# Attention in native float32 on row and column parts of the TensorE array, written as one piece a pair in program order

## The chip, the cores and the metric

The kernel runs on one core of one Trainium2 chip. The metric is the device time of one execution in microseconds (us). The engines that matter are TensorE (PE, with its weight loads shown apart as PEld), VectorE (DVE), ScalarE (ACT), GpSimd (POOL) and SyncE (SP, which only issues DMAs here). Each engine runs its own list of instructions in order and waits on semaphores of the others.

## What is computed

Three blocks follow each other: a linear attention with random features, a gated MLP with a shift in time ("moe"), and a second MLP with a convolution ("moe2"). The change is in the first:

```python
def _attn_ref(q, k, v, w_phi) -> np.ndarray:

    def phi(x):
        proj = np.einsum('bhsd,df->bhsf', x, w_phi)
        proj = proj - np.max(np.abs(proj), axis=-1, keepdims=True)
        return np.concatenate([np.exp(proj), np.exp(-proj)], axis=-1)
    q_p, k_p = (phi(q), phi(k))
    kv = np.einsum('bhsf,bhsd->bhfd', k_p, v)
    z = np.sum(k_p, axis=2)
    num = np.einsum('bhsf,bhfd->bhsd', q_p, kv)
    den = np.einsum('bhsf,bhf->bhs', q_p, z)[..., None] + 1e-06
    return (num / den).astype(np.float32)
```

There are 8 batches, 8 heads, 576 positions, 64 channels a head and 128 features, so 256 with both signs. The moe has 512 channels and 1024 hidden ones: `k = relu(xk @ w_k)`, `v = k*k @ w_v`, `r = sigmoid(xr @ w_r)`, output `r * v`. All is float32.

## The kernel before

Attention works on pairs of heads, `Pi` = 0 to 31, four pairs a batch. For a pair it does these steps on TensorE:

- **Projections** (`project`, lines 242 to 261; `front_k`, `front_q`): q and k of both heads lie transposed in one tile of 128 rows (64 channels a head) and 1152 columns. Nine blocks of 128 columns are multiplied with a block-diagonal weight, 256 output columns for both heads. `BANKS` names the blocks: 5 to 8 are k, 0 to 3 are q, 4 is half q and half k. VectorE takes the maximum of the absolute values (L260) and subtracts it (L265), ScalarE makes exp and exp of the negative (L274, L275, L283, L284).
- **Sums** (`sums`, line 304): `pkv` += k features (128 positions x 128 features as weights) times v with a column of ones (65 columns): 16 products, and 2 of 130 columns for the half block `kr`.
- **Transposes** (`queries`, line 326): the centred q projections are transposed into `pt`, and ScalarE makes the exponentials from there (L345, L346).
- **Numerators** (`numerators`, line 357): 65 weight columns (64 channels and the denominator) times 288 query columns, into `pn`; ScalarE copies them out.
- **`finish`** (line 396) makes reciprocals of the denominators, and `last` (line 410) broadcasts them with a matmul `pr` (L418) and multiplies into `xT`, which the moe reads.

A float32 matmul on this array comes as two records in the trace (two halves of the weights). From pair `NAT` = 6 on the projections, and from pair `NATN` = 8 on the numerators, are not done in float32: operands are split into a rounded part and a rest in the faster `float32r` format (`split`, lines 226 to 240: L235, L236; `queries`: L349, L351, L352; `sums`: L320, L321), and three `float32r` products take the place of one (L256 to L258, and three in L377). The sums stay float32.

The moe (`moe`, line 513 on) is cut into pieces of 12 matmuls of 288 columns by `yield`; each matmul product is also three `float32r` ones (`mm3`, L147 to L149, into `psk`, `psr`, `psv`). The main loop (line 578) steps the attention of a pair and hands out moe pieces by a credit, ten a pair from pair 9 on. The order on each engine is not the order of the code: the framework's scheduler interleaves all instructions, with priority for attention. `order` (line 298) ties only sums and numerators into a chain. After attention the rest of the moe runs, and then moe2 (`psh`, `pso`).

PSUM has eight banks of 2 KB a partition: three in pool `psm` (tag "mm", the moe's and early projections) and five in `psa` (tag "at", attention's).

Of the kernel before, what the change touches and what calls it, by code (L numbers as in the profile page):

```python
# [15 lines left out]
P = 128  # L16
# [6 lines left out]
XT = 6  # L23
# [3 lines left out]
NAT, NATN, PP = 6, 8, 5  # L27
# [17 lines left out]
def fused_kernel(ctx: ExitStack, tc: tile.TileContext, qk, va, wphi, ones2, mu, wk, wv, wr, win, wout, cw, out):  # L45
# [9 lines left out]
    def f(x):  # L55
        return x.bitcast(F32)
# [40 lines left out]
    wph = const.tile([P, 2 * FT], F32R, name="wph")  # L97
    wpl = const.tile([P, 2 * FT], F32R, name="wpl")
    V.tensor_copy(wph, wp0)
    V.tensor_tensor(wpl, wp0, f(wph), ALU.subtract)  # L100

# [52 lines left out]
    with ExitStack() as p1:  # L154
# [45 lines left out]
        loaded, xk, xq, vts = {}, {}, {}, {}  # L200
        KC0 = 512

        def load(Pi):
# [8 lines left out]
            xk[Pi] = (raw,)  # L212
# [5 lines left out]

        def load_half(Pi, k):
            b, p = divmod(Pi, NP)  # L220
            c = slice(KC0, W) if k else slice(0, KC0)
            raw = pool.tile([P, W - KC0], F32, tag="rqk", bufs=1, name="rqk")[:, :c.stop - c.start]
            G.dma_start(raw, qk[b, p, :, c])
            loaded[Pi, k] = raw

        def split(Pi, k):

            raw = loaded.pop((Pi, k))
            if k:
                xh = pool.tile([P, W], F32R, tag="xh", bufs=1, name="xh")  # L230
                xl = pool.tile([P, W], F32R, tag="xl", bufs=1, name="xl")
                xk[Pi] = (xh, xl)
            xh, xl = xk[Pi]
            c = slice(KC0, W) if k else slice(0, KC0)
            A.copy(xh[:, c], raw)  # L235
            V.tensor_tensor(xl[:, c], raw, f(xh[:, c]), ALU.subtract)  # L236
            if k:
                load_half(Pi, False)
            elif Pi + 1 < B * NP:
                load_half(Pi + 1, True)  # L240

        def project(Pi, js):
# [25 lines left out]
        def front_k(Pi):  # L268
            kp = []
            for js in BANKS[:2]:  # L270
                ps, mx = project(Pi, js)
                k_ = pool.tile([P, 2, 2, 2, FT], F32, tag="kp", bufs=2, name="kp")
                t = centred(ps, mx, 2, "tk", 1)
# [30 lines left out]
        def sums(Pi):  # L304
# [8 lines left out]
            if Pi < NATN:  # L313
                kvf = pool.tile([P, 2, 2, V1], F32, tag="kvh", bufs=2, name="kvf")
                A.copy(kvf, pkv)
                kvs[Pi] = (kvf,)
            else:
                kvh = pool.tile([P, 2, 2, V1], F32R, tag="kvh", bufs=2, name="kvh")
                kvl = pool.tile([P, 2, 2, V1], F32R, tag="kvl", bufs=2, name="kvl")
                A.copy(kvh, pkv)  # L320
                V.tensor_tensor(kvl, pkv, f(kvh), ALU.subtract)  # L321
                kvs[Pi] = (kvh, kvl)
# [3 lines left out]
        def queries(Pi, h):  # L326

            t = ts[Pi]
            if Pi < NATN:
                qf = pool.tile([P, 2, S], F32, tag=("qh", "ql")[h], bufs=1, name="qf")  # L330
                q_ = (qf,)
            else:
                qh = pool.tile([P, 2, S], F32R, tag="qh", bufs=1, name="qh")
                ql = pool.tile([P, 2, S], F32R, tag="ql", bufs=1, name="ql")
                q_ = (qh, ql)
            qs[h] = q_
            for o, w, tl in ((0, 384, ((1, 0), (1, 1), (2, 0))), (384, 192, ((2, 1), (0, 0)))):
# [3 lines left out]
                if Pi < NATN:  # L341
                    e = qf[:, :, o:o + w]
                else:
                    e = pool.tile([P, 2, 384], F32, tag="e", bufs=2, name="e")[:, :, :w]
# [392 lines left out]
```

## Time and profile before

| | |
|---|---|
| time, median of 3 runs | 1309.07 us (1306.95 to 1310.03) |
| span of the profiled execution, first to last instruction | 1306.5 us |
| granted TensorE clock | 1.00 of full speed throughout |
| busy PE, DVE, ACT, POOL | 1289.4, 877.0, 797.6, 161.3 us |

The page gives no time of its own for the profiled execution beside its span; the median of the runs is 2.6 us above that span. A busy time sums the records of an engine without counting overlap twice. TensorE's matmuls are pipelined: a record's duration is longer than the time until the next one starts, so the cost of a matmul in a run is read from one start to the next.

### The profile page before, as it was taken

How to read it: one execution, taken by the hardware profiler on the slowest of the kernel's cores; microseconds unless marked ns; L12 is line 12 of the kernel's file. 1: busy time of each engine (PE TensorE's matmuls, PEld its weight loads, DVE VectorE, ACT ScalarE, POOL GpSimd, SP SyncE). 2: the span in 40 equal slices, each digit the busy share in tenths (PEclk: the TensorE clock that was granted, in tenths of full speed). 3: DMA queues.
4: the chain of work that ended last, by engine and by line, in shares of the span. 5: the costliest groups of instructions: out<-in, count | busy, mean ns of one | idle time of the engine just before them, and what ended most of it. 6: DMA issues, size and time to landing. Idle time of an engine off the chain costs nothing.

```text
span 1306.5 us, 25891 instructions
## 1 busy us (share of the span) xinstructions
PE 1289.4 (99%) x9962; PEld 1269.2 (97%) x9962; DVE 877.0 (67%) x1629; ACT 797.6 (61%) x1832; POOL 161.3 (12%) x256
## 2 busy tenths in 40 slices
PE   8899999999999999999999999999999999999998
PEld 7679999999999999999999999999999999999998
DVE  7968887878788778778876844433663553644743
ACT  6877775757667666666775654424564564554653
POOL 6716500111111111011100000000000000000000
PEclk9999999999999999999999999999999999999999
DMA  7313312223332223223221004013102102102100
GB/s 252 116 50 111 106 49 66 73 81 87 100 93 67 86 79 107 74 78 96 79 68 48 21 20 147 19 63 140 64 11 73 41 33 73 37 37 73 37 38 37
DMA packets 74217, 95.76 MB, mean 73 GB/s; under 512 B 26988, under 2 KB 51696, under 8 KB 74096
## 3 DMA queue, kind: packets, MB, share of 16 engines
q1 hardware_dynamic: 60304, 66.26, 16.2%
q0 software_dynamic: 4944, 18.29, 4.7%
q10 hardware_dynamic: 8848, 9.57, 2.6%
q8 instruction: 79, 1.29, 0.4%
q14 instruction: 42, 0.34, 0.1%
HBM read 66.39 MB, written 27.26 MB: 72 GB/s over the span
## 4 chain that ended last, share of the span: by engine, by line
PE 91%; DVE 4%; DMA 2%; ACT 2%; issue 1%; POOL 1%; SPq 0%; DVEq 0%; ACTq 0%; POOLq 0%
PE pn L377 7%; PE pkv L311 6%; PE psh L147 5%; PE psh L148 5%; PE pso L148 5%; PE pso L149 5%; PE psh L149 5%; PE psk L147 5%; PE pso L147 5%; PE psk L149 5%; PE psk L148 5%; PE psv L148 5%; PE psv L149 5%; PE psv L147 5%; PE psr L147 2%; PE psr L149 2%
## 5 line engine op out<-in xcount | busy, mean ns | idle before, releaser
L311 PEld LDWEIGHTS pkv<-va,kp 128*128 128x128 f32 x1024 | 153.9, 191 | 7.5
L148 PE MATMUL psk<-ml,wkh 128*128 128x288 f32 x512 | 152.3, 298 | 0.6 <-DVE ml L492 0.6
L147 PE MATMUL psk<-mh,wkl 128*128 128x288 f32 x512 | 152.7, 299 | 0.0
L311 PE MATMUL pkv<-va,kp 128*128 128x65 f32 x1024 | 152.2, 251 | 0.0
L149 PE MATMUL psv<-kh,wvh 128*128 128x288 f32 x512 | 152.0, 297 | 0.0
L149 PE MATMUL psk<-mh,wkh 128*128 128x288 f32 x512 | 151.6, 296 | 0.0
L148 PE MATMUL psv<-kl,wvh 128*128 128x288 f32 x512 | 151.3, 296 | 0.0
L148 PE MATMUL psh<-xl,wih 128*128 128x288 f32 x512 | 151.1, 296 | 0.0
L147 PE MATMUL psv<-kh,wvl 128*128 128x288 f32 x512 | 150.7, 295 | 0.0
L147 PE MATMUL psh<-xh,wil 128*128 128x288 f32 x512 | 150.6, 296 | 0.0
L149 PE MATMUL psh<-xh,wih 128*128 128x288 f32 x512 | 150.1, 294 | 0.0
L148 PE MATMUL pso<-gl,woh 128*128 128x288 f32 x512 | 148.8, 295 | 0.0
L149 PE MATMUL pso<-gh,woh 128*128 128x288 f32 x512 | 148.7, 295 | 0.0
L147 PE MATMUL pso<-gh,wol 128*128 128x288 f32 x512 | 144.1, 293 | 0.0
L641 DVE SCALAR_TENSOR_TENSOR ct<-h,cw,ct 128x576 f32<-128x576 f32 x64 | 52.4, 819 | 98.0 <-ACT ct L640 97.7
L260 DVE TENSOR_REDUCE mx<-ps 128x4 f32<-128x512 f32 (+1 forms) x160 | 100.0, 628 | 21.5 <-PE ps L258 12.4
L265 DVE TENSOR_TENSOR t<-ps,mx 128x512 f32<-128x512 f32 (+1 forms) x160 | 99.7, 626 | 2.7 <-PE pt L340 2.2
L148 PEld LDWEIGHTS psk<-ml,wkh 128*128 128x128 f32 x512 | 96.2, 188 | 0.8 <-DVE ml L492 0.8
L147 PEld LDWEIGHTS psk<-mh,wkl 128*128 128x128 f32 x512 | 96.1, 188 | 0.4 <-POOL wvl L176 0.3
L149 PEld LDWEIGHTS psv<-kh,wvh 128*128 128x128 f32 x512 | 96.4, 188 | 0.0
L149 PEld LDWEIGHTS psk<-mh,wkh 128*128 128x128 f32 x512 | 96.3, 188 | 0.0
L149 PEld LDWEIGHTS psh<-xh,wih 128*128 128x128 f32 x512 | 96.2, 188 | 0.0
(123 smaller groups left out, 3668.4 us busy)
## 6 DMA issues: line engine op xcount, KB each, us to landing
va<-va SPq DMA_DIRECT2D x32, 325.0 KB, 3.7
x2s<-x SPq DMA_DIRECT2D x32, 288.0 KB, 2.3
x2r<-x2s ACTq DMA_DIRECT2D x32, 288.0 KB, 3.3
out<-ot SPq DMA_DIRECT2D x32, 288.0 KB, 2.1
rqk<-qk POOLq DMA_DIRECT2D x26, 320.0 KB, 3.7
rqk<-qk POOLq DMA_DIRECT2D x26, 256.0 KB, 3.0
raw<-wk SPq DMA_DIRECT2D x8, 512.0 KB, 5.5
raw<-wv SPq DMA_DIRECT2D x16, 256.0 KB, 3.0
```

The source lines that it names most:

```text
L147: T.matmul(ps, wl, xh, start=first, stop=False)
L148: T.matmul(ps, wh, xl, start=False, stop=False)
L149: T.matmul(ps, wh, xh, start=False, stop=last)
L260: V.tensor_reduce(mx, ps, axis=AX.X, op=ALU.max, apply_absolute_value=True)
L265: V.tensor_tensor(t, ps, mx.unsqueeze(3).to_broadcast([P, n, 2, FT]), ALU.subtract)
L311: order(T.matmul(o, k_, v_, start=(i == 0), stop=(i == len(prods) - 1)))
L377: order(T.matmul(pn, kv[a][:, c, h], q_[i][:, c, w], start=(n == 0), stop=(n == len(prods) - 1)))
L641: V.scalar_tensor_tensor(t, h[:, 1:S + 1], cw0[:, fc, 1:2], t, ALU.mult, ALU.add)
```

## The change

From pair `SW` = 6 on attention is done by new functions. All splitting is gone, and every product is float32 with tiles that cover a part of the array:

- `rows`: a projection of one head uses the 64 rows of its channels and 128 weight columns; the two heads lie in the two row halves and write different banks.
- `sums4`: each product is cut into four of 32 weight columns, which write 32 partitions each.
- `numerators4`: the 64 channels of the two heads are four strips of 32 columns; the denominators are products of their own (`pd`), with the last 32 of the 65 columns as weights.
- `block(Pi)` writes a pair's whole TensorE work as one piece: the broadcast of the pair before, the transposes of `Pi`, projections of k for `Pi + 2` and q for `Pi + 1`, sums of `Pi + 1`, numerators of `Pi`. The main loop hands out ten moe pieces behind it, and TensorE runs all of this in program order (`manual_schedule`); the other engines are still scheduled. `finish` comes at step `FS` = 4 of 15.
- Pairs up to 5 stay as they are, and pair 6's projections are made by the old code over full rows, in float32.

```diff
-NAT, NATN, PP = 6, 8, 5
+SW, PP = 6, 5
+NS, FS = 15, 4
...
-                if len(x) == 1:
-                    T.matmul(o, x[0][:, c], wp0, start=True, stop=True)
-                else:
-                    T.matmul(o, x[1][:, c], wph, start=True, stop=False)
-                    T.matmul(o, x[0][:, c], wpl, start=False, stop=False)
-                    T.matmul(o, x[0][:, c], wph, start=False, stop=True)
+                T.matmul(o, x[:, c], wp0, start=True, stop=True)
...
+        def rows(Pi, prods):
+
+            x = xk[Pi]
+            for o, h, j in prods:
+                r = slice(D * h, D * h + D)
+                T.matmul(o, x[r, j * P:j * P + P], wp0[r, h * FT:h * FT + FT], start=True, stop=True)
+
+        def rows_last(Pi):
+            ps = [psa.tile([P, 4, FT], F32, tag="at", name="p1") for _ in range(2)]
+            rows(Pi, [(ps[h][:, 0], h, 4) for h in range(2)])
...
+        def rows4(Pi, j0, nm):
+            ps = [psa.tile([P, 4, FT], F32, tag="at", name=nm) for _ in range(2)]
+            rows(Pi, [(ps[h][:, j], h, j0 + j) for j in range(4) for h in range(2)])
+            return ps
...
+        def sums4(Pi):
...
+            for i, (o, k_, v_) in enumerate(prods):
+                for r in range(0, P, 32):
+                    T.matmul(o[r:r + 32], k_[:, r:r + 32], v_, start=(i == 0), stop=(i == len(prods) - 1))
...
+        def queries4(Pi):
+
+            t1, *tq = ts[Pi]
+            qf = [pool.tile([P, 2, S], F32, tag=("qh", "ql")[h], bufs=1, name="qf") for h in range(2)]
+            for h in range(2):
+                pt = psm.tile([P, 512], F32, tag="mm", name="pt")
+                for j in range(4):
+                    T.transpose(pt[:, j * P:j * P + P], tq[j // 2][:, j % 2, h] if Pi == SW else tq[h][:, j], ident)
+                for c in range(2):
+                    A.activation(qf[h][:, c, :512], pt, AF.Exp, scale=1.0 - 2 * c)
+            pt = psm.tile([P, 512], F32, tag="mm", name="pt")
+            for h in range(2):
+                T.transpose(pt[:, h * P:h * P + P], t1[:, 0, h], ident)
...
+        def numerators4(Pi, qf):
...
+                for c in range(2):
+                    for r in range(4):
+                        h, o = r // 2, 32 * (r % 2)
+                        T.matmul(pn[32 * r:32 * r + 32], kv[:, c, h, o:o + 32], qf[h][:, c, w], start=(c == 0), stop=(c == 1))
+                A.copy(u[:, hf], pn)
+            pd = psa.tile([P, 512], F32, tag="at", name="pd")[:, :HS]
+            for c in range(2):
+                for r in range(4):
+                    h, hf = divmod(r, 2)
+                    T.matmul(pd[32 * r:32 * r + 32], kv[:, c, h, V1 - 32:], qf[h][:, c, hf * HS:hf * HS + HS], start=(c == 0), stop=(c == 1))
...
+        def block(Pi):
+
+            nq, nk = Pi + 1 < B * NP, Pi + 2 < B * NP
+            run_late()
+            qf = queries4(Pi)
+            if nk:
+                rows_last(Pi + 2)
+                tk = centre4(rows4(Pi + 2, 5, "pk"), "tk")
+            if nq:
+                ts[Pi + 1] += centre4(rows4(Pi + 1, 0, "pq"), "tq")
+                del xk[Pi + 1]
+                sums4(Pi + 1)
+            numerators4(Pi, qf)
+            if nk:
+                features(Pi + 2, tk)
+                load_v(Pi + 2)
+            if Pi + 3 < B * NP:
+                load(Pi + 3)
...
+        with tc.manual_schedule(engines={mybir.EngineType.PE}):
+            for Pi in range(SW, B * NP):
+                for n, _ in enumerate(attention4(Pi)):
+                    extras(Pi, n)
+                    feed(Pi)
+            run_late()
```

How TensorE's list reads, first before, in the middle of a pair late in the attention. `pn` are numerators, `pkv` sums (with weights `kp`, and `kr` for the half block), `ps` projections, `pt` transposes:

```order
L377 MATMUL pn<-ql,kvh 65x288
L311 MATMUL pkv<-va,kr 128x130
L377 MATMUL pn<-qh,kvh 65x288
L311 MATMUL pkv<-va,kr 128x130
L256 MATMUL ps<-wph,xl 128x256
L257 MATMUL ps<-wpl,xh 128x256
L258 MATMUL ps<-wph,xh 128x256
L256 MATMUL ps<-wph,xl 128x256
L257 MATMUL ps<-wpl,xh 128x256
L258 MATMUL ps<-wph,xh 128x256
L340 MATMUL pt<-ident,t 128x128 x2
L256 MATMUL ps<-wph,xl 128x256
```

Numerators and sums of different pairs alternate one by one, transposes stand between projections, and moe matmuls stand between such groups.

TensorE after the change, at the head of a pair's piece, behind the last moe matmul, with the engines that an instruction waits for:

```order
L145 MATMUL psk_6285<-mh0_5759,wkh_103 128x288
L361 MATMUL pr_6301<-rr_108,on2_81 128x288 [waits DMAHW6_49,DMAHW1_49,DMAHW7_49,DMAHW0_49,PE_49]
L361 MATMUL pr_6304<-rr_108,on2_81 128x288 [waits PE_49]
L484 MATMUL pt_6309<-ident_69,t_5971 128x128 [waits Activation_49]
L484 MATMUL pt_6309<-ident_69,t_5971 128x128 x3
L484 MATMUL pt_6316<-ident_69,t_5975 128x128 [waits Activation_49]
L484 MATMUL pt_6316<-ident_69,t_5975 128x128 x3
L489 MATMUL pt_6323<-ident_69,t_5518 128x128 [waits PE_49,Activation_49]
L489 MATMUL pt_6323<-ident_69,t_5518 128x128
L422 MATMUL p1_6330<-wp0_74,rqk_6104 128x128 [waits DMASW5_49]
L422 MATMUL p1_6331<-wp0_74,rqk_6104 128x128
```

The broadcasts and all ten transposes now stand together ahead of the projections, and the third `pt` tile waits for ScalarE, which reads the first. Both lie in one bank in 20 of the 26 pieces.

TensorE after the change, further on in a piece, from the last sums to the denominators (two or eight products of one row stand in different strips):

```order
L473 MATMUL pkv_6795<-va_6500,kp_6489 32x65 x8
L473 MATMUL pkv_6795<-va_6500,kp_6492 32x65 x8
L473 MATMUL pkv_6795<-va_6500,kr_6495 32x130 x8
L505 MATMUL pn_6871<-qf_6725,kvf_6450 32x288 x2
L505 MATMUL pn_6871<-qf_6726,kvf_6450 32x288 x2
L505 MATMUL pn_6871<-qf_6725,kvf_6450 32x288 x2
L505 MATMUL pn_6871<-qf_6726,kvf_6450 32x288 x2
L505 MATMUL pn_6881<-qf_6725,kvf_6450 32x288 x2
L505 MATMUL pn_6881<-qf_6726,kvf_6450 32x288 x2
L505 MATMUL pn_6881<-qf_6725,kvf_6450 32x288 x2
L505 MATMUL pn_6881<-qf_6726,kvf_6450 32x288 x2
L511 MATMUL pd_6891<-qf_6725,kvf_6450 32x288 x2
```

Sums stand in one run and numerators in another, four neighbouring products in four strips. Each product is two matmuls with a weight load each in the built program, and the two of one strip stand next to each other.

## Rows read from the trace of the kernel before

**Rows 1.** The page: span, busy time and share of TensorE, granted clock in 40 slices, chain.
```profile
span 1306.5 us, 25891 instructions
...
PE 1289.4 (99%) x9962; PEld 1269.2 (97%) x9962; DVE 877.0 (67%) x1629; ACT 797.6 (61%) x1832; POOL 161.3 (12%) x256
...
PEclk9999999999999999999999999999999999999999
...
PE 91%; DVE 4%; DMA 2%; ACT 2%; issue 1%; POOL 1%; SPq 0%; DVEq 0%; ACTq 0%; POOLq 0%
```

**Rows 2.** Windows (us: length, busy time by engine and records, clock, DMA): attention, moe2.
```profile
387.80:495.20 107.40, 107.40 (x878) 107.40 (x878) 86.75 (x182) 73.17 (x182) 14.99 (x20) 1.00 0.30 85
...
905.00:1306.00 401.00, 397.73 (x3003) 397.49 (x3001) 213.98 (x284) 216.60 (x408) 5.94 (x58) 1.00 0.14 45
```

**Rows 3.** Timeline of TensorE (start, duration), the half block's sums four pairs apart.
```profile
387.77 0.38 PE L311 MATMUL pkv<-va,kr 128*128 128x130 f32 x2
...
495.19 0.38 PE L311 MATMUL pkv<-va,kr 128*128 128x130 f32 x2
```

**Rows 4.** Timeline of TensorE in the early pairs, dense runs of float32 records.
```profile
22.28 0.71 PE L340 MATMUL pt<-ident,t 128*128 128x128 f32 x5
22.83 0.56 PE L311 MATMUL pkv<-va,kp 128*128 128x65 f32 x4
...
23.71 0.78 PE L311 MATMUL pkv<-va,kp 128*128 128x65 f32 x6
24.33 1.95 PE L254 MATMUL ps<-wp,rqk 128*128 128x256 f32 x8
26.11 0.65 PE L377 MATMUL pn<-qf,kvf 128*65 128x288 f32 x2
...
36.83 1.62 PE L377 MATMUL pn<-qf,kvf 128*65 128x288 f32 x6
38.28 0.33 PE L311 MATMUL pkv<-va,kp 128*128 128x65 f32 x2
```

**Rows 5.** Timeline of TensorE around 505 us: split products alone and among sums.
```profile
503.26 0.29 PE L377 MATMUL pn<-qh,kvh 128*65 128x288 f32 x1
503.39 0.29 PE L377 MATMUL pn<-qh,kvl 128*65 128x288 f32 x1
...
505.60 0.33 PE L311 MATMUL pkv<-va,kp 128*128 128x65 f32 x2
505.74 0.33 PE L377 MATMUL pn<-qh,kvh 128*65 128x288 f32 x1
505.90 0.33 PE L311 MATMUL pkv<-va,kp 128*128 128x65 f32 x2
...
507.55 0.28 PE L256 MATMUL ps<-wph,xl 128*128 128x256 f32 x1
507.67 0.28 PE L257 MATMUL ps<-wpl,xh 128*128 128x256 f32 x1
```

**Rows 6.** Groups by line and shape: count, busy us, mean ns, idle before.
```profile
L260 DVE TENSOR_REDUCE mx<-ps 128x4 f32<-128x512 f32 x128 | 87.4, 684 | 21.5 <-PE ps L258 12.4 <-PE ps L254 8.9
L265 DVE TENSOR_TENSOR t<-ps,mx 128x512 f32<-128x512 f32 x128 | 86.6, 679 | 2.6 <-PE pt L340 2.2
...
L352 DVE TENSOR_TENSOR ql<-e,qh 128x768 fp32r<-128x768 f32 x48 | 45.3, 945 | 0.3
...
L274 ACT ACTIVATE kp<-t 128x512 f32<-128x512 f32 x64 | 40.4, 632 | 30.7 <-DVE t L265 30.1 <-PE pkv L311 0.5
...
L236 DVE TENSOR_TENSOR xl<-rqk,xh 128x640 fp32r<-128x640 f32 x26 | 21.2, 817 | 0.0
```

**Rows 7.** DMA issues on the page: KB each, us from issue to landing.
```profile
rqk<-qk POOLq DMA_DIRECT2D x26, 320.0 KB, 3.7
```

More of the change, by code (lines that the diff above doesn't have):

```diff
@@ L312, in sums @@
                 yield
[L313 to L322, printed above, removed]
+            kvs[Pi] = pool.tile([P, 2, 2, V1], F32, tag="kvh", bufs=2, name="kvf")
+            A.copy(kvs[Pi], pkv)
         ts, kps_, kvs, late = {}, {}, {}, []
@@ L328, in queries @@
             t = ts[Pi]
[L329 to L336, printed above, removed]
+            qs[Pi, h] = qf = pool.tile([P, 2, S], F32, tag=("qh", "ql")[h], bufs=1, name="qf")
             for o, w, tl in ((0, 384, ((1, 0), (1, 1), (2, 0))), (384, 192, ((2, 1), (0, 0)))):
@@ L374, in numerators @@
                 w = slice(hf * HS, hf * HS + HS)
-                prods = [(c, a, i) for c in range(2) for a, i in (((1, 0), (0, 1), (0, 0)) if len(kv) == 2 else ((0, 0),))]
-                for n, (c, a, i) in enumerate(prods):
-                    order(T.matmul(pn, kv[a][:, c, h], q_[i][:, c, w], start=(n == 0), stop=(n == len(prods) - 1)))
-                    share[0] += 18 / (3 * len(prods)) if h or hf else 0
+                for c in range(2):
+                    order(T.matmul(pn, kv[:, c, h], qf[:, c, w], start=(c == 0), stop=(c == 1)))
+                    share[0] += 3 if h or hf else 0
                     while share[0] >= 1:
@@ new lines, in centre4, with features @@
+        def centre4(ps, tag):
+            out_ = []
+            for h in range(2):
+                out_.append(pool.tile([P, 4, FT], F32, tag=tag, bufs=2, name="t"))
+                centre(ps[h], out_[h])
+            return out_
+        def features(Pi, tk):
+            kp = kps_[Pi] = []
+            for h in range(2):
+                k_ = pool.tile([P, 4, 2, FT], F32, tag="kp", bufs=2, name="kp")
+                A.activation(k_[:, :, 0], tk[h], AF.Exp)
+                A.activation(k_[:, :, 1], tk[h], AF.Exp, scale=-1.0)
+                kp.append(k_)
+            k_ = pool.tile([P, 2, FT], F32, tag="kr", bufs=1, name="kr")
+            for h in range(2):
+                r = slice(64 * h, 64 * h + 64)
+                A.activation(k_[r, 0], ts[Pi][0][64:, 0, h], AF.Exp)
+                A.activation(k_[r, 1], ts[Pi][0][64:, 0, h], AF.Exp, scale=-1.0)
+            kp.append(k_)
@@ new lines, in sums4 @@
+        def sums4(Pi):
+            kp, vt = kps_.pop(Pi), vts.pop(Pi)
+            pkv = psa.tile([P, 2, 2, V1], F32, tag="at", name="pkv")
+            prods = [(pkv[:, c, h], kp[h][:, i, c], vt[:, i, h]) for i in range(4) for h in range(2) for c in range(2)]
+            prods += [(pkv[:, c], kp[2][:, c], vt[:, 4]) for c in range(2)]
+            for i, (o, k_, v_) in enumerate(prods):
+                for r in range(0, P, 32):
+                    T.matmul(o[r:r + 32], k_[:, r:r + 32], v_, start=(i == 0), stop=(i == len(prods) - 1))
+            kvs[Pi] = pool.tile([P, 2, 2, V1], F32, tag="kvh", bufs=2, name="kvf")
+            A.copy(kvs[Pi], pkv)
@@ L480, in mix, with attention4 @@
+        def attention4(Pi):
+            for n in range(NS):
+                if n == 0:
+                    while late and done[0] * NP <= Pi - 1 - XT:
+                        next(m)
+                    block(Pi)
+                if n == FS:
+                    finish(Pi)
+                yield
         def mix(u, j):
@@ L576, in fused_kernel, with extras, feed @@
         load(1)
-        credit = 0
-        for Pi in range(-1, B * NP):
+        def extras(Pi, n):
+            if wsteps and n in WAT.get(Pi, ()):
+                wsteps.pop(0)()
+            if Pi == 7 and n == 14:
+                taps()
+            if Pi >= DS0 and dsteps and n in (3, 11):
+                dsteps[0] = dsteps[0][0](), dsteps[0][1]
+            if Pi >= DS0 and dsteps and n in (4, 12):
+                raw, step = dsteps.pop(0)
+                step(raw)
+        def feed(Pi):
+            if Pi >= MS:
+                credit[0] += (10 if Pi >= SLOW else SR[Pi]) / 15
+                while credit[0] >= 1:
+                    credit[0] -= 1
+                    next(m, None)
+        credit = [0]
+        for Pi in range(-1, SW):
             it = attention(Pi)
```

105 lines of the change are left out of this document (45 added, 60 removed).

## The prediction

> **What bounds the kernel now.** Read the page first. TensorE (PE) is busy 99% of the 1306.5 us span, always at the full granted clock, and carries 91% of the chain that ended last [rows 1]. VectorE and ScalarE are busy about two thirds of the time, so what they gain or lose counts only where TensorE waits for them. Then the stretches: between 387.8 and 495.2 us TensorE has no idle time at all, DVE works 86.75 us of the 107.4 and ACT 73.17 [rows 2]. So in this stage time is the sum of what TensorE's instructions take, and the question is what each kind of matmul takes from one start to the next (its own duration, 0.29 us or so, overlaps that of the next).
>
> The repeating unit of the stage is four pairs. The same two-record `kr` group starts at 387.77 and at 495.19 us [rows 3]: 107.42 us for four pairs, and in them four times ten MLP pieces of 12 matmuls, 480 in all. An MLP matmul takes 401.0/3003 = 0.1335 us, by the last stretch, where nothing else runs [rows 2]; 480 of them take 64.1 us. The other 43.3 us are attention: **10.8 us a pair**. The change touches 26 of them (pairs 6 to 31).
>
> **What the parts of a pair take.** A full float32 product stands in the trace as two records. From dense runs [rows 4]: a record with 288 columns takes (38.28-36.83)/6 = 0.242 us, one with 256 columns (26.11-24.33)/8 = 0.22, a transpose of 128 columns (22.83-22.28)/5 = 0.11. That is 0.84 ns a column, so a record of 65 columns would need 0.055; yet six `pkv` records take (24.33-23.71)/6 = 0.103. In such a run the load of 128 weight columns sets the pace, not the streaming. The split products (three records in place of two) run at 0.12 for 256 columns and 0.13 for 288 [rows 5]; where a `pkv` pair and a `pn` alternate, the three take 0.30 (505.60 to 505.90).
>
> **What the change removes.** Per pair 27 split projections (27 x 0.12 = 3.2 us), 24 split numerators (3.1), the 36 `pkv` records woven between them, and their changes of kind. All of that is the 10.8 with 10 transposes (1.1) and 2 `pr` (0.26). Off TensorE it removes the splitting itself: of VectorE's rows alone, L352's and L236's larger forms are 45.3 and 21.2 us in all [rows 6]. This is worth nothing directly, since TensorE did not wait for it; it is the cover for what follows.
>
> **What it adds, per pair.** The transposes and `pr` stay: 1.36 us. *Projections:* 18 products of 64 rows and 128 columns, 36 records at 0.11 (a transpose's width). Neighbours in the program lie in different row halves; if halves run side by side, 18 x 0.11 = 2.0 us, if not 4.0. *Sums:* 64 products of 32 weight columns and 65 moving ones and 8 with 130, so 128 x 0.055 + 16 x 0.11 = 8.8 us laid end to end, 2.2 if the four column strips run side by side. *Numerators and denominators:* 16 + 8 products, 48 records x 0.242 = 11.6 us end to end, 2.9 side by side. No row of this kernel shows two matmuls in the array at once, so the ends are 2.0 + 2.2 + 2.9 = 7.1 us and 24.4. I take the low end: the operands, weights and output partitions of neighbours are disjoint, and nothing in the program orders them. That is the choice on which the forecast stands. (The Trainium skill, "TensorE: Matmul & The Clock Gate", Part 3, gives 2.38 times for three column strips and 3.07 for four row strips; no run here shows it.)
>
> *Changes of array shape:* three a pair (whole to halves, halves to strips, strips to whole). The trace has none. The ends are nothing, and an empty pipe plus one load: a record lasts 0.29 and the next starts 0.13 later [rows 5], so 0.16 us of tail, and 0.10 for the weights [rows 4], 0.26 x 3 = 0.78. I take 0.7, near the upper end, since the next shape's weights can hardly lie in a part still in use. (The skill's "TensorEngine Tiling (Array Packing)", Tiling Modes, says that a change of mode drains the engine; by it the upper end would stand, 0.08 us a pair more.)
>
> *A new wait:* in 20 of the 26 pieces the built program puts the third `pt` tile into the bank of the first, since the MLP holds the third bank of that pool. Its two transposes wait until both exponentials of the first tile are done: 0.16 tail + 2 x 0.63 (L274 has the same width [rows 6]) - 0.44 for the second tile's transposes = 0.98 us. Behind them in TensorE's program order stands everything else, so it is lost: 0.98 x 20/26 = 0.75 a pair. *Other waits in the piece:* the exponentials need some 0.9 + 4 x 0.63 + 4 x 0.3 = 4.6 us from the piece's start, and the numerators start after 1.4 + 1.0 + 2.0 + 2.2 = 6.6, so they are hidden by 2 us. VectorE must empty the projection banks before `pn` and `pd` take them. The last of these needs about 0.4 + 0.9 + 1.6 + 2.7 + 1.4 = 7.0 us by rows L260, L265 [rows 6], and TensorE gets there after about 9. Both covers end if MLP work (mixing, casts) stands ahead in those queues; I put 0.3 on it, with ends 0 and 2.0. *DMAs:* the next q/k load is issued on POOL after the piece and lands in 3.7 us [rows 7], and a pair lasts over 20, so nothing. The sums' load and the denominators' four small DMAs on SP have as much room.
>
> **The sum.** 1.36 + 7.1 + 0.7 + 0.75 + 0.3 = 10.2 us against 10.8: -0.6 a pair, -15.6 for 26. Pair 6's projections go over whole rows, 18 x 0.22 against 27 x 0.12: +0.7. The profiled span of 1306.5 becomes 1291.6. The runs' median is 2.6 us above that span, so **1294 us**. With its own unknowns (waits 0 to 1.0, shapes 0 to 0.78) this case runs from 1268 to 1315.
>
> **Rivals.**
> 1. *Matmuls do not pass each other, and the two records of one float32 product need the same strip* (slower). The built program has the two halves of one strip next to each other. If the second half must wait for the first, and whatever is behind it waits too, only the second half of one strip and the first half of the next overlap: 24 x 0.242 = 5.8 for the numerators, 64 x 0.055 + 8 x 0.11 = 4.4 for the sums, 2.1 for the projections, 12.3 in place of 7.1. That is +5.2 - 0.6 = 4.6 a pair, +120: 1430 us. It decides as soon as overlap stays below about 3 strips. For it: in every stretch read here matmuls start in the order of the program. Against it: no row shows a strip at all. (The Trainium skill's clock-gate page, Part 3, states it as a rule: matmuls start and end in program order, and only weight loads are pulled ahead.)
> 2. *Strips compute side by side, but weights load one after another* (slower). At the pace of the dense `pkv` run, 0.103 for 128 columns, the 36 projection loads take 3.7 us and the 144 loads of 32 columns 3.7: +3.2 - 0.6 = 2.6 a pair, 1378 us. For it: that run is bound by loads. Against: loads into different parts need not share a path.
> 3. *The parts run one after another*, the change not doing what it says: 24.4 in place of 7.1, +17.3 - 0.6 = 16.7 a pair, 1743 us.
> 4. *Waits of the piece in program order eat the gain* (slower): before, a late VectorE or ScalarE was covered by any ready matmul; now nothing passes. From 0.9 us a pair on it decides; at 2.0 it gives 1338 us. For it: DVE is 81% busy in this stage [rows 2]. Against: some 6 us of splitting a pair leave that engine.
>
> **How the numbers follow.** The forecast has 0.55, rival 1 0.20, rival 2 0.10, rival 3 0.05, rival 4 0.10. About 0.2% is what a measurement of this kernel can tell from no change (2.6 us). Of the forecast's 0.55, 0.45 lies below 1306.5, 0.05 within 0.2% and 0.05 above; rival 4 gives 0.01 to no change. So faster 0.45, same 0.06, slower 0.49: the likeliest case is faster, but the others nearly all lie on the other side. The range leaves out rival 3 and the far sides of the forecast and of rival 1: 1265 to 1438, and beside it the forecast's own 1268 to 1315.
>
> **What would show it.** In the changed profile: a pair's piece some 10 us long; numerator records starting 0.06 us apart on average (0.12 under rival 1, 0.24 under rival 3), sums' records 0.015 apart (0.03 under rivals 1 and 2), projections 0.055; idle of about a microsecond ahead of the third `pt`, released by ScalarE; a four-pair cycle of 105 us. The forecast is wrong if numerator records stand 0.12 or more apart, or if idle time ahead of the piece's parts passes 2 us a pair.

## The result, and the profile after

| | before | after |
|---|---|---|
| median, lowest to highest | 1308.76 us (1306.95 to 1310.03) | 1314.97 us (1314.85 to 1317.39) |
| ratio, 95% interval | | 1.0055 (1.0041 to 1.0069) |
| span of the profiled execution | 1306.5 us | 1313.2 us |

The change makes the kernel half a per cent slower, about three times what a measurement can tell from no change. The forecast was 1294, faster.

The page of the changed kernel, with the lines that answer to [rows 1]:

```profile
span 1313.2 us, 32577 instructions
...
PE 1263.1 (96%) x13518; PEld 1193.4 (91%) x13518; DVE 760.0 (58%) x1457; ACT 710.7 (54%) x1654; POOL 136.8 (10%) x230
...
PEclk9998899999999999999999999999999999999999
...
PE 86%; DVE 4%; ACT 3%; issue 3%; DMA 2%; POOL 1%; SPq 0%; DVEq 0%; POOLq 0%; ACTq 0%
```

TensorE is busy 26.3 us less than before, though it runs a third more matmuls; VectorE and ScalarE have 117 and 87 us less to do. Yet the span is 6.7 us longer: TensorE now stands idle 50 us in place of 17. And the clock, which was full throughout, dips in the fourth and fifth slice, from about 98 to 164 us.

**A steady piece.** The timeline of TensorE in one pair's piece (start, duration of the group, tile, shape, count; idle before it and who ended that):

```profile
531.50 0.43 PE L361 MATMUL pr<-rr,on 128*128 128x288 f32 x2
531.77 1.03 PE L484 MATMUL pt<-ident,t 128*128 128x128 f32 x8
533.54 0.44 PE L489 MATMUL pt<-ident,t 128*128 128x128 f32 x2 [0.74 <-ACT qf L486]
533.91 0.49 PE L422 MATMUL p<-wp,rqk 64*128 64x128 f32 x4
534.23 1.06 PE L422 MATMUL pk<-wp,rqk 64*128 64x128 f32 x16
535.13 1.26 PE L422 MATMUL pq<-wp,rqk 64*128 64x128 f32 x16
536.32 2.03 PE L473 MATMUL pkv<-va,kp 128*32 128x65 f32 x128
538.17 0.62 PE L473 MATMUL pkv<-va,kr 128*32 128x130 f32 x16
538.62 2.26 PE L505 MATMUL pn<-qf,kvf 128*32 128x288 f32 x32
540.56 1.29 PE L511 MATMUL pd<-qf,kvf 128*32 128x288 f32 x16
541.78 0.40 PE L143 MATMUL psv<-kh,wvl 128*128 128x288 f32 x1
```

From one start to the next this reads: 16 `pk` records in 0.90 us, 0.056 apart; 128 `pkv` records in 1.85, 0.0145 apart; 32 numerator records in 1.94, 0.061 apart. Two row halves and four column strips do run side by side, at the paces the forecast named. (The 16 `pq` records do it less well: they take 1.19 us, with one half starting late and ending alone.) The single records show how: four `pn` records of four strips start at 538.616, .619, .629 and .632 us, the next four at 538.858 and after, 0.242 behind them. The records carry no number of their strip; that the four lie in four strips is concluded from their starts, since records of this width in one part of the array start 0.242 us apart [rows 4]. In the program the two records of one strip are neighbours, so the second of them is passed by the first ones of the other strips.

**Where the time went.** To compare stages that hold different amounts of moe work, take the time at which the last sums (`kr`) of a pair start, less 0.1335 us [rows 2] for each moe matmul started by then; what is left is attention with all its waits. In the new form this mark comes 1.94 us of work too early: the numerators and denominators of the pair before are still to come (3.16 us in the piece above), and the next pair's k projections are done (1.22); in the old form it is the other way round. From pair 7 on these 1.94 us are added.

After minus before, this is +1.9 us at pair 5's sums and +2.6 at pair 6's, which are still old code, +14.0 at pair 7's, made in the first new piece, +10.4 at pair 11, +7.3 at pair 30, and +6.8 at the last attention matmul, which is the whole difference of the spans. The first 1.9 us are not the change's: in the twelve runs below, which have the same code up to there, pair 5 stands between -1.4 and +1.6. So the entry into the new order lost 11 us at once and had lost 8 by pair 11, and the 19 pairs from 11 to 30 won back 3.1, 0.17 us a pair.

**The entry.** The timeline of TensorE from pair 5's last numerators (`pn`) into the first piece (pair 6):

```profile
113.31 0.65 PE L320 MATMUL pn<-qf,kvf 128*65 128x288 f32 x2
...
119.78 0.29 PE L145 MATMUL psk<-mh,wkh 128*128 128x288 f32 x1
126.69 0.82 PE L361 MATMUL pr<-rr,on 128*128 128x288 f32 x2 [6.62 <-DMA rr<-r]
127.31 1.91 PE L484 MATMUL pt<-ident,t 128*128 128x128 f32 x8
...
134.36 2.04 PE L422 MATMUL pq<-wp,rqk 64*128 64x128 f32 x14 [3.02 <-DVE t L441]
136.33 3.69 PE L473 MATMUL pkv<-va,kp 128*32 128x65 f32 x128
```

The piece begins with `pr`, the broadcast of pair 5's reciprocals. These are not there yet, and nothing behind `pr` passes it: 6.62 us of idle. The next wait is 3.02 us for VectorE. The windows of this stretch (length; PE, PEld, DVE, ACT, POOL busy; clock):

```profile
120.00:124.00 4.00, 0.07 (x1) 0.00 (x0) 4.00 (x14) 3.26 (x9) 2.58 (x3) 0.89 0.20 62
124.00:128.00 4.00, 1.31 (x6) 1.32 (x7) 2.36 (x6) 1.92 (x5) 3.45 (x3) 0.50 0.50 141
128.00:132.00 4.00, 3.35 (x30) 2.82 (x28) 3.97 (x8) 3.62 (x9) 3.39 (x4) 0.75 0.26 64
132.00:136.00 4.00, 1.64 (x14) 1.67 (x14) 4.00 (x12) 2.99 (x10) 1.06 (x1) 0.67 0.27 82
136.00:140.00 4.00, 4.00 (x135) 3.77 (x137) 4.00 (x8) 0.34 (x1) 1.35 (x2) 0.50 0.49 146
```

Behind each of the two waits the granted clock is 0.50, the lower of the two levels (1.2 in place of 2.4 GHz); between them it is up for a while. Behind the second one the `pkv` run takes 3.69 us in place of 2.03. From `pr` to the next moe matmul this piece lasts 16.77 us, where a quiet one without the wait for the bank takes 9.18: 3.02 us are the wait for VectorE, and some 4.6 are runs that take longer, most of them at the lower clock. With the 6.62 us ahead of `pr` that is 14.2. VectorE is full. Why the reciprocals are late stands in its timeline:

```profile
120.17 0.15 DVE L343 TENSOR_SCALAR den<-den 96x12 f32<-96x12 f32 x1
...
121.17 0.21 DVE L344 RECIPROCAL rd<-den 96x12 f32<-96x12 f32 x1
121.31 0.62 DVE L440 TENSOR_REDUCE mx<-pk 128x4 f32<-128x512 f32 x1
121.85 0.40 DVE L72 SCALAR_TENSOR_TENSOR hc<-raw,hc 128x256 uint32<-128x256 uint32 x1
...
122.38 0.36 DVE L346 CAST r<-rd 96x12 fp32r<-96x12 f32 x1
...
123.59 0.16 DVE L347 TENSOR_TENSOR r<-rd,r 96x12 fp32r<-96x12 f32 x1
```

Four small steps of `finish` stand between maxima (L440, L441) and the conversion of moe weights (L70 to L72) and take 3.6 us. With ScalarE's copies and the transfer of the denominators ahead and that of the reciprocals behind, the chain lasts 12.7 us, from the end of the last numerators (113.31 + 0.65) to `pr`. TensorE had 6.1 us of other work behind them, up to 119.78 + 0.29.

**The waits** of TensorE over the whole run (waiter, releaser: us in all, times, longest):

```profile
PE pt L489 <- ACT qf L486: 14.8, 20, 0.7
PE pr L361 <- DMA rr<-r: 6.9, 2, 6.6
...
PE pq L422 <- DVE t L441: 4.6, 3, 3.0
...
PE pkv L473 <- issue: 3.6, 6, 1.6
```

### The profile page after: what moved, and what is told of

Read it like the earlier page. It is cut to its first block, busy times and chain, and to the rows that moved or that the text cites. A ratio compares the mean times of both kernels' runs of the same rounds, so it can differ in the third digit from the quotient of the medians.

```text
span 1313.2 us, 32577 instructions
## 1 busy us (share of the span) xinstructions
PE 1263.1 (96%) x13518; PEld 1193.4 (91%) x13518; DVE 760.0 (58%) x1457; ACT 710.7 (54%) x1654; POOL 136.8 (10%) x230
## 4 chain that ended last, share of the span: by engine, by line
PE 86%; DVE 4%; ACT 3%; issue 3%; DMA 2%; POOL 1%; SPq 0%; DVEq 0%; POOLq 0%; ACTq 0%
PE psh L143 5%; PE psh L144 5%; PE psv L143 5%; PE pso L144 5%; PE pso L145 5%; PE psh L145 5%; PE pso L143 5%; PE psv L144 5%; PE psv L145 5%; PE psk L143 5%; PE psk L145 5%; PE psk L144 5%; PE pkv L473 5%; PE pn L505 4%; PE psr L143 3%
## 5 line engine op out<-in xcount | busy, mean ns | idle before, releaser
L610 ACT ACTIVATE kf<-psk 128x288 f32<-128x288 f32 x128 | 52.6, 412 | 96.3 <-PE psk L145 96.0
L143 PEld LDWEIGHTS psv<-kh,wvl 128*128 128x128 f32 x512 | 96.1, 188 | 8.2 <-issue 6.0
L612 DVE TENSOR_TENSOR kf<-kf 128x576 f32<-128x576 f32 x64 | 48.5, 757 | 83.4 <-ACT kf L610 82.7
L144 PEld LDWEIGHTS psv<-kl,wvh 128*128 128x128 f32 x512 | 96.2, 188 | 0.0
```

What stands on the lines that cost most here:

```text
L143: T.matmul(ps, wl, xh, start=first, stop=False)
L144: T.matmul(ps, wh, xl, start=False, stop=False)
L610: A.activation(kf[:, j], ps, AF.Relu)
L612: V.tensor_tensor(kf, kf, kf, ALU.mult)
```

## The experiments

Two theories stood at the start. **A:** parts run side by side as forecast, and the gain went to two things, the entry at pair 6 and waits inside a piece in program order. **B**, in several forms: the gain of the parts is itself smaller than it looks, or what a wait takes is lost in some other way if the wait is removed.

### 1. The broadcast moved away from the head of the first piece

```diff
-            run_late()
+            if Pi > SW:
+                run_late()
...
             numerators4(Pi, qf)
+            if Pi == SW:
+                run_late()
```

> Edit: in the first piece (pair 6) the broadcast of pair 5 is moved from the head of the piece to its end; nothing else. Theory A (the loss lies at the entry into program order: TensorE stood 6.6 us at the first piece's head for the denominators' DMA of pair 5, and the clock fell to half behind that wait): the wait and most of the half-clock stretch go, 7 to 13 us, so 1302 to 1308 us. Theory B (the loss lies in the pieces of the steady stage, and the wait at the entry only delays work that VectorE's and GpSimd's weight conversion would hold up anyway): 1312 to 1316 us.

Measured: 1311.14 us, ratio 1.0016 (1.0004 to 1.0028). The 6.6 us wait is gone, and at pair 7 the kernel is 2.0 us behind the one before by the measure above, in place of 14.0 (the profiled execution took 1307.67 us, less than the median). But at pair 9 it is 4.9 behind: TensorE has waited 2.0 us for ScalarE at 149.7 us, and the clock falls to 0.81 and 0.76 in the windows from 148 to 156 us. So 3.8 us came of it in place of 7 or more, and the time lies between the ranges of A and B: the head was one cause of the entry's loss, and the same crowded stretch had others behind it.

### 2. The third transposed tile in another bank

```diff
+            pt = psa.tile([P, 512], F32, tag="at", name="pt")
+            for h in range(2):
+                T.transpose(pt[:, h * P:h * P + P], t1[:, 0, h], ident)
...
             for h in range(2):
                 pt = psm.tile([P, 512], F32, tag="mm", name="pt")
...
-            pt = psm.tile([P, 512], F32, tag="mm", name="pt")
-            for h in range(2):
-                T.transpose(pt[:, h * P:h * P + P], t1[:, 0, h], ident)
```

(With its exponentials, which move along: the half block's tile comes from the attention's pool and is made first.)

> Edit: the third transpose tile of a piece is taken from attention's PSUM pool and made first, so that it shares no bank with the first. Theory A: the 0.74 us wait on ScalarE goes in 20 of 26 pieces, 14.8 us in all; some comes back where the projections now wait for that bank, so 1300 to 1306 us. Theory B (the wait is only moved: VectorE or ScalarE is late for the next step in the piece by the same amount): 1311 to 1316 us.

Measured: 1299.1 us, ratio 0.9931 (0.9917 to 0.9944). The wait for ScalarE is gone from the list, and an undisturbed piece takes 9.18 us in place of 10.14. That 0.96 us in 20 pieces is what the forecast had at 0.98. The time is 15.9 us lower and just below A's range. TensorE's waits in this run:

```profile
PE pr L361 <- DMA rr<-r: 6.7, 2, 6.5
PE pq L422 <- DVE t L441: 5.4, 4, 2.3
```

The entry's waits are as they were, so this is a cause of its own.

### 3. Both edits

> Both edits. Theory A (the two losses are independent and on the path): the sum of both gains, 1288 to 1298 us, below the kernel before (1308.8). Theory B: above 1306 us.

Measured: 1297.56 us, ratio 0.9915 (0.9902 to 0.9928). That is at the slow end of what both causes together should give: with the bank changed, moving the broadcast brings 1.5 us, less than half of what it brought alone. By the measure, counted from pair 6, it is 7.8 us ahead of run 2 at pair 7 and 2.8 at pair 11: most of what left the head came back in the next pieces. Waits without a visible releaser grow from 5.0 to 7.8 us in `pkv`, those for VectorE in `pq` do not (5.4 and 4.9).

### 4. The scheduler in place of program order

```diff
-        with tc.manual_schedule(engines={mybir.EngineType.PE}):
+        with ExitStack():
```

> Edit: TensorE's order is left to the scheduler again (no manual order), all products still on row and column parts. Theory A (one piece a pair is needed: each change of the array's shape costs some 0.1 to 0.2 us, 0.45 us for the three of a piece, and mixing with MLP matmuls makes tens of changes a pair): 1350 us or more. Theory B (program order costs more by its waits than it saves in changes of shape): below 1310 us.

Measured, one run: 1333.59 us. Between the two numbers; the sign is A's. By the measure the entry costs far less here: attention falls back by 2.6 us from pair 6 to pair 7, in place of 11.3. But from pair 11 to 30 it falls back by 20.0 more, where the changed kernel wins 3.1. In the stretch from 400 us on the scheduler puts moe matmuls between transposes, projections and sums, so that a pair changes array shape more often. Program order thus costs about 9 us at its entry and is worth 1.2 us a pair behind it, some 19 us in the net.

### 5. Neighbours in the same part

```diff
-                for c in range(2):
-                    for r in range(4):
+                for r in range(4):
+                    for c in range(2):
...
-            rows(Pi, [(ps[h][:, j], h, j0 + j) for j in range(4) for h in range(2)])
+            rows(Pi, [(ps[h][:, j], h, j0 + j) for h in range(2) for j in range(4)])
```

(The loops of the denominators turn likewise.)

> Same work as the changed kernel, but neighbours in the program now lie in the same part of the array: all four records of one strip stand together in numerators and denominators, all eight records of one row half in the projections (sums as they were). Theory A (each part of the array has matmuls of its own waiting, and they start as soon as their part is free, however far back in the program): numerators stay at 1.9 to 2.1 us and denominators at 1.1 a piece, four records still start within 0.02 us of each other, and the time stays within 4 us of the changed kernel's 1315. Theory B (only the next two or three instructions of the program are looked at, and the overlap seen is owed to neighbours lying in different parts): a strip's records run one after another and only the ends overlap with the next strip, so numerators take 3.2 to 4.6 us, denominators 1.6 to 2.3 and the projections 3.6 to 4.0: +2.8 to +5 us a pair, 1380 to 1440 us.

Measured, one run: 1324.89 us, between the ranges of the two theories. Numerators take 1.94 and denominators 1.15 us, as A has it: four strips start at 409.487, .494, .506 and .520 us, though the fourth strip's first record is the thirteenth in the program: it starts ahead of nine earlier ones. The projections are between the two:

```profile
404.22 0.49 PE L422 MATMUL p<-wp,rqk 64*128 64x128 f32 x4
404.55 1.27 PE L422 MATMUL pk<-wp,rqk 64*128 64x128 f32 x13
...
405.99 1.27 PE L422 MATMUL pq<-wp,rqk 64*128 64x128 f32 x13
407.19 2.03 PE L473 MATMUL pkv<-va,kp 128*32 128x65 f32 x128
```

From `p` to the sums it is 2.97 us in place of 2.41: the second half, eight records back, starts when the fifth record of the first one does, and so passes three. So matmuls from far back in the program pass others, but not without limit; what sets the limit, and why the strips reach further than the halves, stays open.

### 6. The sums over the whole array

```diff
-                for r in range(0, P, 32):
-                    T.matmul(o[r:r + 32], k_[:, r:r + 32], v_, start=(i == 0), stop=(i == len(prods) - 1))
+                T.matmul(o, k_, v_, start=(i == 0), stop=(i == len(prods) - 1))
```

> The sums (key features times values) of pairs 7 to 31 go over the whole array again, 18 float32 products of 128 weight columns in place of 72 of 32; projections and numerators stay in parts. Theory A (the strips of the sums gain what the arithmetic of the forecast says): 36 records at the 0.103 us of the dense early run take 3.7 to 4.0 us against the 2.3 of the changed kernel, +1.4 to +1.7 a pair for 25 pairs, 1350 to 1358 us. Theory B (strips save nothing here, their loads or the change of array shape eat it): the sums' stage stays at 2.2 to 2.6 us and the time within 8 us of 1315.

Measured, one run: 1354.96 us, as A has it. The sums in this run:

```profile
393.20 3.79 PE L472 MATMUL pkv<-va,kp 128*128 128x65 f32 x32
...
397.42 2.15 PE L504 MATMUL pn<-qf,kvf 128*32 128x288 f32 x32
```

4.22 us from the first sum to the first numerator against 2.30, a little over what A expected. Strips take 1.9 us off an undisturbed piece (10.14 against 12.08). In the stretch from 265 to 750 us they bring only 1.45 on the mean, 10.64 against 12.09: this run's pieces are all alike, and the changed kernel's vary from 10.1 to 12.0 us. So the many short records have a price of about 0.5 us a pair there. Between 230 and 780 us this run has no wait "issue" in a piece at all, the changed kernel 4.2 us.

What TensorE waits for there can be read from the traces. Its instructions seem to come by the DMA queue that the pages list as q8, "instruction": the bytes go with the number of PE and PEld records, 64 or 65 a record before, after and in this run. The line of the page before, then after (packets, MB, share):

```profile
q8 instruction: 79, 1.29, 0.4%
...
q8 instruction: 106, 1.74, 0.6%
```

In the piece from 291.2 us on, one of these packets (16 KB each) takes from 296.17 to 297.80 us, and the sums of the changed kernel stand still until 1.27 us behind its end:

```profile
296.03 1.92 PE L473 MATMUL pkv<-va,kp 128*32 128x65 f32 x120
299.07 0.32 PE L473 MATMUL pkv<-va,kp 128*32 128x65 f32 x8 [1.12 <-issue]
```

In the changed kernel's pieces 8 waits of 0.15 us or more have no visible releaser, in those of the other eleven runs in program order 83; all 91 end 1.18 to 1.61 us behind the end of a packet of this queue. The changed kernel's 19 pieces from 265 to 746 us take 9.6 us more than 19 quiet ones, and 8.6 of these are lost in the 1.9 us behind such a packet (the profile puts two of these waits, 1.2 us, on VectorE). The sums have 288 records, matmuls and weight loads, in 2.3 us; in this run they have 72 in 4.2, and no such wait. No run changes the supply alone; that late instructions are the cause rests on this close coincidence in time.

### 7. The new form from pair 8

```diff
-SW, PP = 6, 5
+SW, PP = 8, 5
```

(on top of the second experiment)

> The variant with the third transposed tile in another bank (1299.1 us), and the new form starts with pair 8 in place of pair 6; pairs 6 and 7 run as before the change. Two pairs in the old form cost about 1.6 us each against the new form of that variant, +3.2. Theory A (the loss at the entry comes from VectorE, which splits the MLP's first weights while the first two pieces ask for it, and from the clock that falls then; two pairs later these splits are over): the wait on VectorE (about 5 us) and the stretch at half clock go, the wait for the reciprocals' transfer at the head of the first piece (6.6 us) stays but is the only loss: 1294 to 1299 us. Theory B (the entry costs the same wherever it lies, since the wait at its head itself lets the clock fall): 1301 to 1304 us, with the granted clock at about 0.5 after the first piece's head.

Measured: **1286.92 us**, ratio 0.983 (0.9814 to 0.9846), better than either theory. The clock is 1.00 in every stretch, and no piece has a wait above 1.05 us. Even the wait that A left in place is gone. The chain on VectorE, then on SyncE, then TensorE from the last old numerators to the head of the first piece, three cuts of the timeline:

```profile
158.78 0.17 DVE L343 TENSOR_SCALAR den<-den 96x12 f32<-96x12 f32 x1 [3.80 <-DMA den<-dn]
...
159.44 0.16 DVE L346 CAST r<-rd 96x12 fp32r<-96x12 f32 x1
159.64 0.17 DVE L347 TENSOR_TENSOR r<-rd,r 96x12 fp32r<-96x12 f32 x1
```

```profile
156.17 0.54 SPq L335 DMA_DIRECT2D den<-dn  x1
159.63 2.63 SPq L349 DMA_DIRECT2D rr<-r  x4
```

```profile
154.40 0.65 PE L320 MATMUL pn<-qf,kvf 128*65 128x288 f32 x2
...
168.06 0.44 PE L361 MATMUL pr<-rr,on 128*128 128x288 f32 x2
```

VectorE is free and does the four steps in 1.0 us, and TensorE has 13.0 us of work (155.05 to 168.06) between the last numerators and `pr`, where at pair 6 it had 6.1. The chain takes some 9 here: to 162.3 for the last of the four issues, and about 2 for landing. This wait is gone because the work in front of it is longer than the chain.

### 8. The same with the broadcast moved

> As the run before (new form from pair 8, third transposed tile in another bank), and the broadcast of the last old-form pair's reciprocals moved from the head of the first piece to its end. Theory A (VectorE's splits of weights and the wait at the head are separate causes, and only with the splits over does removing the wait pay in full): about 6 us below the run before, 1288 to 1293 us, no wait above 2 us in the first three pieces and the clock at 0.95 or more from pair 8 on. Theory B (what is taken from the head comes back in the next pieces, as in the two runs where it was tried at pair 6): within 2 us of the run before.

Measured: 1287.25 us, ratio 0.984 (0.9825 to 0.9854): no difference. The expectation rested on a wait that run 7 no longer has, so there was nothing to remove.

### 9. The changed kernel from pair 8, nothing else

> The changed kernel with one number altered: the new form starts with pair 8 in place of pair 6 (the third transposed tile stays in the bank that waits). Theory A (the new form is worth something in every pair even with its wait, and the entry at pair 6 alone turned that into a loss): the variant with the other bank lost 12.2 us when the entry moved two pairs (1299.1 to 1286.9); here two pairs give up only some 0.4 us each in place of 1.1, so 11 to 14 us off 1315: 1301 to 1304, which is 5 to 8 us below the kernel before. Theory B (without the other bank the steady pairs gain nothing, and what the entry took would have been lost by the end anyhow): 1308 us or more.

Measured: 1302.59 us, ratio 0.9963 (0.995 to 0.9976), in the middle of A's range. One number turns the change from 0.55% slower to 0.37% faster. Moving the entry by two pairs is worth 12.4 us, and `pr` now waits 0.4 us in the whole run.

### 10. Two pairs later still

> The fastest variant so far (new form from pair 8, other bank, 1286.9 us) with the new form from pair 10. Theory A (at pair 8 the entry no longer costs anything, so a later entry only gives up two more pairs at 1.1 us, the slope of that run against the kernel before): 1288 to 1291 us. Theory B (some of the entry's loss is still there at pair 8): 1286 us or less.

Measured: 1297.11 us, ratio 0.9915 (0.9902 to 0.9927). A miss for both: 10 us slower than from pair 8. One part is a reckoning that was wrong. In the changed kernel pairs before the switch are whole-array float32, not split, and in this run the sums of pairs 9 and 10 come 12.7 and 12.8 us of attention behind those of the pair before, where the kernel before has 10.8 late in the attention. From the sums of pair 8 to those of pair 11 run 7 takes 9.6 a pair, so a pair given up costs 3.2 us, not 1.1: 6.4 of the 10. Of the rest, 2.3 us are lost between the sums of pairs 10 and 11, in the first new piece, and 1.3 were there at pair 8's sums, up to which both runs have the same code.

### 11. Weight conversions out of pairs 5 and 6

```diff
-WAT = {... 5: range(0, 17, 2), 6: range(0, 15, 2)}
+WAT = {... 5: (0,), 6: (), 7: range(0, 15, 2), 8: range(0, 15, 2)}
```

> The changed kernel with the steps that split the moe's first weights (loads on SyncE's queue, three passes on VectorE each) taken out of pairs 5 and 6 and spread over pairs 7 and 8, or done when the moe asks for them; the entry stays at pair 6. Theory A (what makes the first piece wait is these splits, which stand between the small VectorE steps that make pair 5's reciprocals and behind which the projections' maxima queue): the wait for the reciprocals' transfer falls from 6.6 to under 4 us and the wait of the second piece for VectorE from 3.0 to under 1.0; 1308 to 1313 us if the moe does not then wait for its weights, and the moe's own waits for weights, 2 us in the changed kernel, grow to at most 6, which gives the rest back: 1308 to 1317. Theory B (the wait is the length of the chain itself, four small transfers, four VectorE steps and four transfers more, with nothing on TensorE to cover it): it stays at 6 us or more, and the time at 1313 or more.

Measured: 1334.73 us, ratio 1.0207 (1.0179 to 1.0234). TensorE's waits:

```profile
PE psv L143 <- POOL wvl L172: 11.9, 7, 3.5
...
PE pr L361 <- DMA rr<-r: 7.3, 2, 6.9
...
PE pq L422 <- DVE t L441: 1.6, 2, 0.8
```

The long wait for VectorE in the projections is gone, as A had it. The wait at the head is not: 6.9 us, theory B. The chain was again drawn out on VectorE (its four steps from 114.93 to 120.65 us), this time by mixing and squares of the moe in place of conversions; and TensorE's other work behind the last numerators lasted 5.7 us (110.9 to 116.6), with `pr` at 123.5. The moe then waits for its weights far more than expected, and from 148 to 172 us the clock stays at 0.50. So conversions explain the second wait. The first needs no conversions, only too little TensorE work in front, and a full VectorE queue makes it longer: with VectorE free the chain takes some 9 us in run 7, and against the 6.1 us of work at pair 6 about 3 of the 6.6 would stay (an estimate from these two runs).

### 12. The new form from pair 7

> The variant with the other bank for the third transposed tile, entry at pair 7, between the runs at pair 6 (1299.1) and pair 8 (1286.9). Theory A (the entry's loss follows how much of VectorE's splitting is still to come): the waits at the head are between those of the two, 1287 to 1296 us, and the granted clock stays above 0.9 in every 4 us stretch from the head of the first piece on. Theory B (it is the kind of pair, odd or even, or chance of the order): outside that range.

Measured: 1293.09 us, ratio 0.9877 (0.9857 to 0.9897), within A's time. `pr` does not wait, but A's other half fails: a wait of 2.1 us for ScalarE in the first piece and one of 2.3 for the moe's weights remain, and the clock falls to 0.57 for 8 us at 148 us.

## Why the prediction was wrong

**Right: what the parts of a pair take.** Projections, sums, numerators and denominators were put at 2.0, 2.2 and 2.9 us; 2.41, 2.29 and 3.16 stand in the piece above, the array's changes of shape included. These were put at 0.7 in all: a change from whole array to halves and one from halves to strips each show 0.20 us to the next start where 0.11 is the pace, and the change back shows 0.34 behind a strip's last record where 0.085 to 0.24 is. That is some 0.3 to 0.45 a piece. (The drain of the engine that the Trainium skill states in "TensorEngine Tiling (Array Packing)", Tiling Modes, would fit these longer distances; they are smaller than the 0.78 worked out for it.) An undisturbed piece with the bank's wait takes 10.14, one without 9.18. Weighted with 20 of 26 that is 9.92, and the forecast without its "other waits" has 9.9.

**Right: the choice on which it stood.** Rivals 1, 2 and 3 fall with the record starts (0.061, 0.0145 and 0.056 apart) and with runs 5 and 6. For rival 1 stood a rule of the Trainium skill ("TensorE: Matmul & The Clock Gate", Part 3), that matmuls start and end in the order of the program. Here they do not: with the two records of one strip adjacent in the program, the first records of all four strips start within 16 ns, and in run 5 a strip starts whose first record is the thirteenth in line. That holds for disjoint parts of the array; no run shows whole-array matmuls that pass each other.

**Wrong, the first step: the entry was priced at +0.7.** The forecast summed 26 steady pairs and one term for pair 6's projections. That the new order begins with a matmul which waits on a chain through two transfers and four VectorE steps, with 6.1 us of other TensorE work in front, was in no term. By the measure above attention is 10.4 us behind at pair 11, 1.9 of them from ahead of the entry; the other 8.5 stand where the sum had -2.3 (five pairs at -0.6, and +0.7): 10.8 of the 21 us between forecast and result. Runs 7 and 9 put the price of the place at 12 us, and run 9 shows the sign of the result hangs on it.

**Wrong, the second step: "other waits 0.3, with ends 0 and 2.0".** From pair 11 to 30 the mean piece takes (372.8 - 169.8)/19 = 10.68 us by the same measure, against 10.85 for before: a gain of 0.17 and not 0.6. The quiet piece is as forecast, and two terms are not. The wait for the bank, 0.75 a pair in the sum, stands in 18 of these 19 pieces and takes 0.91 here; over all 26 pieces its size was right. The other waits take 0.55 us on the mean in place of 0.3, and most of that is not what the term was made for: it priced late VectorE and ScalarE, and the runs show TensorE standing still until just behind the landing of its own instructions (run 6), which was in no term. Over these 19 pairs the shortfall is 8 of the 21 us. With the 1.9 us from ahead of the entry that makes the 21.

**Luck.** The time lies at the upper end of the forecast's own range, 1268 to 1315, but not for the range's reasons: that end was made of changes of shape and of waits in every pair, and half of the error came from one place. The range also took other waits only to 1.0 us, where the working had named 2.0 as their end.

**Rival 4** named this mechanism (nothing passes a late VectorE or ScalarE) and its place, inside the pieces. It set the deciding point at 0.9 us in each pair. In the pieces it never got there, and what disturbed them most was not a late VectorE or ScalarE; it was decided at one place, the entry, which is worth 12 us. The shown evidence against it, the splitting work that VectorE loses, was taken from the steady stretch and says nothing about a stretch where this engine is full.

## What to carry to other kernels

Disjoint parts of the array are worth pricing as running side by side, and a hand-written order that keeps one shape together is worth 1.2 us a pair here once it runs, some 19 in the net. But where such an order begins after a scheduled stretch, first find the longest chain that its head waits for and count the independent work in front of it: moving the switch by two pairs was worth 12.4 us, nearly as much as the best edit inside the piece (15.9). That edit was to give each tile a bank that no engine still reads: one shared bank took 0.96 us in each of 20 pieces. And count instructions where products are cut into many short ones: their supply took about 0.5 us a pair here.

Together, switch at pair 8 and a bank of its own give 1286.92 us, 1.7% below the kernel before and 2.1% below the changed one.

## What the hardware showed that was not expected

- Float32 matmuls in different column strips pass each other: in run 5 the thirteenth record of the program starts 33 ns behind the first, ahead of nine earlier ones. For row halves the ninth starts only with the fifth, ahead of three.
- At the entry the granted clock fell to 0.50 during the wait of 6.6 us, stood at 0.75 and 0.67 in the windows from 128 to 136 us, and fell to 0.50 again behind a wait of 3.0 us; in the window from 140 us on it was 0.97. In run 11 it stayed at 0.50 from 148 to 172 us, while TensorE was busy 16.9 of the 24.
- TensorE can stand still for its own instructions: all 91 waits of 0.15 us or more that no semaphore explains, in pieces with 144 short records of sums, end 1.18 to 1.61 us behind a 16 KB packet of the queue "instruction". With 36 records (run 6) there is none, and all pieces from 276 to 726 us take 12.08 or 12.09 us. With 144 records but pieces that are 0.63 us longer when quiet (run 5) there are 3.
